# Sending k's column maxima through memory instead of through TensorE

## The chip, the cores and the metric

The kernel runs on one NeuronCore of a Trainium2 chip. The core has five engines with an instruction queue each: PE (TensorE; the profile shows its weight loads apart, as PEld), DVE (VectorE), ACT (ScalarE), POOL (GpSimd) and SP (SyncE, which here only starts transfers). Each engine works through its own queue in order and waits on semaphores for the others. The metric is device time in microseconds, from one launch to its end; lower is better.

## The reference

Linear attention over 8 batches x 8 heads, 576 positions and 64 columns per head, and behind it a mixer of two small networks. All of it is float32.

```python
q_s = q - np.max(q, axis=-1, keepdims=True)
q_s = np.exp(q_s)
q_s = q_s / (np.sum(q_s, axis=-1, keepdims=True) + 1e-09)
k_s = k - np.max(k, axis=2, keepdims=True)        # the maximum over the 576 positions
k_s = np.exp(k_s)
k_s = k_s / (np.sum(k_s, axis=2, keepdims=True) + 1e-09)
kv = np.einsum('bhsd,bhse->bhde', k_s, v)
attn = np.einsum('bhsd,bhde->bhse', q_s, kv)
...
xt = x.transpose(0, 2, 1)                          # x: attn, its heads side by side
h = np.maximum(xt @ w_tok1, 0.0) @ w_tok2
u = x + h.transpose(0, 2, 1)
h2 = np.maximum(u @ w_ch1, 0.0) @ w_ch2
out = u + h2
```

The softmax of k runs along the positions, so its maximum is one number per column of k.

## The kernel before, in words

Two heads of one batch are a unit, so that 2 x 64 columns fill 128 partitions. There are 32 units. For each the kernel loads q and k with the positions on the partitions (five chunks of 128 rows), k also transposed (`kt`, columns on the partitions), and v. Units 0 to 7 are the early ones; units 8 to 13 come next; from unit 14 on (`PAIRED` = 14), units are treated in pairs: `stage_kv` of both units of a pair stands at the pair's first place.

The second network (the channel network, `ch1` and `ch2`) works on groups of 512 rows. A group needs 12 steps, one for each 128 of the 1536 hidden channels. In a step, `ch1` does 12 matmuls of 512 columns into one bank of `ps_h` (L430). ACT empties that bank into `h2h` (L433), DVE into `h2l` (L434), the rest that `h2h` lacks, so that two reduced-precision products stand for a float32 one. `ch2` of the step before then does 12 matmuls into the four banks of `ps_o` (L442). After a group's last step `out_end` empties those four banks on DVE (L473, L474), and ACT starts the stores. The units' own stages are put between the steps: the dictionary `todo`, filled by `put`, says at which step, or half a step later, a stage is traced.

k's softmax is `softmax_k`. From unit 8 on it does this: DVE reduces `kt` along the row to one maximum per column, `mc`, one per partition (L237). The product needs those 128 numbers along the free axis, in every partition alike. So ACT scales the identity by `mc` into `dg` (L251), PE multiplies a matrix of ones with `dg` (L253; a float32 product, two instructions in the trace), and ACT copies the result from its bank to `mb` (L254). POOL subtracts `mb` from k (L255), and ACT takes the exponential (L256). `stage_kv` (L295) uses the result. `dg` and `mb` are one buffer each, `mc` has two, and `kt` has one (L154).

q's softmax (`softmax_q`) begins with a reduction on DVE that waits for q's load (L263), and ends with the split into `qh` and `ql`, the latter on POOL (L118). Then DVE and ACT turn q block by block (L344).

The order on each engine is not the order of the text. A planner (`schedule_with_timeline_sim=True`) takes the traced instructions, with their place in the text as priority, and writes each engine's queue by its own estimate of when things are ready. `tc.issue_after(ins)` adds an edge for it without a semaphore: instructions traced inside the block that stand on the engine of `ins` come behind `ins` in that engine's queue. `behind(...)` (L417) does so for a list of instructions, and `drained` (L432) holds the two emptyings, on ACT and on DVE, of the last `ch1` traced.

Of the kernel before, what the change touches and what calls it, by code (L numbers as in the profile page):

```python
# [8 lines left out]
F32 = mybir.dt.float32  # L9
F32R = mybir.dt.float32r  # L10
U32 = mybir.dt.uint32
AF = mybir.ActivationFunctionType
# [3 lines left out]
P = 128  # L16
# [4 lines left out]
def attn_mixer_kernel(ctx: ExitStack, tc: tile.TileContext, q, k, kt, v, wt, out, dims):  # L21
# [3 lines left out]
    nc = tc.nc  # L25
# [12 lines left out]
    PAIRED = NE + NJ + 2  # L38
# [5 lines left out]
    sm = ctx.enter_context(tc.tile_pool(name="sm", bufs=2))  # L44
# [6 lines left out]
    ident = const.tile([P, P], F32R, name="ident")  # L51
# [13 lines left out]
    ones = const.tile([P, P], F32, name="ones")  # L65
# [26 lines left out]
    dg = lay.tile([P, P], F32, name="dg")  # L92
    for i in range(3):
        slots[i][1] = lay.tile([P, NJ, CW], F32R, name=f"ul{i}")
    mb = lay.tile([P, P], F32, name="mb")
# [14 lines left out]
    Q = 32  # L110

    def f32(ap):
        return ap.bitcast(F32)
# [8 lines left out]
    def ps_unit(dtype=F32):  # L122

        pools = unit_banks[0]
        pool, name = pools[turn[0] % len(pools)]
        turn[0] += 1
        return pool.tile([P, 512], dtype, name=name)
# [102 lines left out]


    turned_k = []

    def softmax_k(u):
        ktt = u["kt"]
        mc = sm.tile([P, 1], F32, name="mc")
        nc.vector.tensor_reduce(mc, ktt, axis=AX.X, op=ALU.max)  # L237
        kx = u["k"]
        if u["early"]:
            nc.vector.tensor_scalar(mc, mc, -1.0, None, op0=ALU.mult)  # L240
            nc.scalar.activation(ktt, ktt, AF.Exp, bias=mc)
            t = ps_unit()
            for c in range(C):
                nc.tensor.transpose(t[:, c * P : (c + 1) * P], ktt[:, c * P : (c + 1) * P], f32(ident))
            nc.scalar.copy(kx[:, 0:C, :], t.rearrange("p (c d) -> p c d", c=C))
            t = ps_unit()
            turned_k.append(nc.tensor.transpose(t[:, 0:P], ktt[:, S0 : S0 + P], f32(ident)).ins)
            nc.scalar.copy(kx[:, C, :], t[:, 0:P])
            return

        nc.scalar.activation(dg, f32(ident), AF.Copy, scale=mc)  # L251
        t = ps_unit()
        nc.tensor.matmul(t[:, 0:P], ones, dg, start=True, stop=True)  # L253
        nc.scalar.copy(mb, t[:, 0:P])  # L254
        nc.gpsimd.tensor_tensor(kx, kx, mb.unsqueeze(1).broadcast_to([P, C1, P]), op=ALU.subtract)  # L255
        nc.scalar.activation(kx, kx, AF.Exp)  # L256

# [30 lines left out]
    def stage_kv(u):  # L288
        kx, vt = u["k"], v_of[u["n"]]
        kv = ps_unit()  # L290

        for c in range(C1):
            for h in range(2):
                hs = slice(h * D, (h + 1) * D)
                nc.tensor.matmul(kv[hs, 0 : D + 1], kx[:, c, hs], vt[:, c, h, :], start=(c == 0), stop=(c == C))  # L295

        if u["n"] != NE - 1 and u["n"] < PAIRED:
            load_v(u["n"] + 2 if u["n"] < NE else u["n"] + 1)
        rs = sm.tile([P, 1], F32, name="rs")
        nc.vector.tensor_scalar(rs, kv[:, D : D + 1], 1e-9, None, op0=ALU.add)  # L300
        nc.vector.reciprocal(rs, rs)
        kvf = kv_ring[u["n"] % len(kv_ring)]
        for h in range(2):
            hs = slice(h * D, (h + 1) * D)
            nc.scalar.activation(kvf[hs, hs], kv[hs, 0:D], AF.Copy, scale=rs[hs])
        u["kvf"] = kvf
        if not u["early"] and u["n"] < PAIRED:
            split_kv(u)

    def split_kv(u):  # L310
        kvf = u["kvf"]
        kvh = wk.tile([P, P], F32R, name="kvh")
        kvl = wk.tile([P, P], F32R, name="kvl")
        split(kvh, kvl, kvf, nc.vector)
        u["kvh"], u["kvl"] = kvh, kvl
# [67 lines left out]
    def stage_u(u, half):  # L383
        b, j = u["b"], u["j"]
        edge = (b + 1) * CW - b * S
        cut = min(max(edge, S - 320), 320)
        n0, n1 = ((0, cut), (cut, S))[half]
        N = n1 - n0
        ns = slice(n0, n1)
        t = ps_unit()  # L390
        if u["early"]:
            mm = [(u["kvf"], u["qt"][:, ns])]
        else:
            mm = [(u["kvh"], u["qth"][:, ns]), (u["kvh"], u["qtl"][:, ns]), (u["kvl"], u["qth"][:, ns])]
        for n in range(NT):
            mm += [
                (u["hh"][:, n, :], w2h[:, n, ns]),
                (u["hh"][:, n, :], w2l[:, n, ns]),
                (u["hl"][:, n, :], w2h[:, n, ns]),
            ]  # L400
        for i, (a, w) in enumerate(mm):
            nc.tensor.matmul(t[:, 0:N], a, w, start=(i == 0), stop=(i == len(mm) - 1))  # L402
        for g, a0, a1 in ((b, n0, min(n1, edge)), (b + 1, max(n0, edge), n1)):
            if a0 < a1:
                at = b * S + a0 - g * CW
                uh, ul = (x[:, j, at : at + a1 - a0] for x in uT[g])
                src = t[:, a0 - n0 : a1 - n0]
                emptied[:] = [
                    nc.scalar.copy(uh, src).ins,  # L409
                    nc.vector.tensor_tensor(ul, src, f32(uh), op=ALU.subtract).ins,  # L410
                ]


    drained = []

    @contextmanager
    def behind(instructions):  # L417
        with ExitStack() as stack:
            for ins in instructions:
                stack.enter_context(tc.issue_after(ins))  # L420
            yield
# [56 lines left out]
    units = {}  # L478

    def begin(n):  # L480
        if n < NU and n not in units:
            units[n] = load_unit(n // NJ, n % NJ)

    def soft(n):
        if n < NU:
            softmax_k(units[n])
            softmax_q(units[n])

    def pe_stages(n):
        def s1():  # L490
            stage_qT(units[n])
            stage_kv(units[n])

        def s2():
            stage_y(units[n])

        def s3():
            stage_h1(units[n])
            stage_u(units[n], 0)

        def s4():
            stage_u(units[n], 1)

        return s1, s2, s3, s4
# [66 lines left out]

    todo = {}


    def second_places():
        t = part.rearrange("p n c -> p (n c)")
        n = C1 * 2 * (D + 1)
        v_ring.append(v_places(t[:, 0:n].rearrange("p (c h e) -> p c h e", c=C1, h=2)))
        nc.gpsimd.memset(t[:, n : n + P], 0.0)
        kv_ring.append(t[:, n : n + P])  # L580
        load_v(PAIRED + 1)
# [6 lines left out]
    def put(at, fn):  # L588
        todo.setdefault(int(2 * at) / 2, []).append(fn)
# [4 lines left out]
    for n in range(NE, NU):  # L594
        b, j = divmod(n, NJ)
        s1, s2, s3, s4 = pe_stages(n)
        if b == 2:
            at = (n0 - 10, n0 - 9, n0 - 9, n0 - 7.5) if j == 0 else [n0 - 9.5 + 2 * j + x for x in (0, 0.5, 1, 1.5)]
            put(at[0], s1)
            put(at[0], lambda n=n: soft(n + 1))  # L600
            put(at[0] + 0.5, lambda n=n: begin(n + 2))
            for x, fn in zip(at[1:], (s2, s3, s4)):
                put(x, fn)
            continue
        at = n0 + (b - 3) * NF + 3 * j - 1
        if prev is not None:
            put(at, lambda n=prev: (stage_u(units[n], 0), stage_u(units[n], 1)))
        if n < PAIRED:
            put(at, lambda n=n: (stage_kv(units[n]), stage_y(units[n]), stage_qT(units[n])))
        elif n % 2 == 0:  # L610
            put(at, lambda n=n: (stage_kv(units[n]), stage_kv(units[n + 1]), load_v(n + 2), load_v(n + 3)))
            put(at, lambda n=n: (split_kv(units[n]), stage_y(units[n]), stage_qT(units[n])))
        else:
            put(at, lambda n=n: (split_kv(units[n]), stage_y(units[n]), stage_qT(units[n])))
        if n + 1 < PAIRED:
            put(at, lambda n=n: soft(n + 1))
        elif n + 1 < NU:
            put(at, lambda n=n: softmax_q(units[n + 1]))
        put(at + 0.5, lambda n=n: begin(n + 2))

        for m, x, y in ((n + 2, 0.5, 1.5),) if n < PAIRED else ((n + 2, 0.5, 1.5), (n + 3, 2, 3)) if n % 2 == 0 else ():
            if m < NU:
                put(at + x, lambda m=m: (begin(m), load_kt(units[m])))
                put(at + y, lambda m=m: softmax_k(units[m]))
        if n + 2 >= PAIRED and n + 2 < NU:
            put(at + 0.5, lambda n=n: load_q(units[n + 2]))
        if n + 1 == PAIRED:
            put(at - 1, second_places)
        put(at + 1.5, lambda n=n: stage_h1(units[n]))
        prev = n  # L630
# [88 lines left out]
```

## Time and profile before

| | us |
|---|---|
| median of three runs | 816.17 (814.79 to 816.81) |
| profiled execution | 816.05 |
| its span, first to last instruction | 814.2 |
| mean granted TensorE clock | 0.992 |

| engine | busy us | instructions |
|---|---|---|
| PE | 797.4 | 4512 |
| PEld | 678.8 | 4512 |
| DVE | 495.4 | 1104 |
| ACT | 338.2 | 898 |
| POOL | 84.2 | 72 |

A row of groups reads: line, engine, operation, tiles written and read, shape, count, then busy time, the mean of one in ns, and the idle time of the engine just before, with what ended it. A row of waits reads: who waited for whom, the sum in us, how often, the longest. A row of the timeline gives start and length in us, and in brackets the idle time before. Matmuls are pipelined, so a matmul's length in the profile is more than what it adds to the time; the difference of two starts shows that.

The 24 products of L253 start between 145.4 and 606.1 us; six belong to units 8 to 13, and the eighteen from 245.8 us on to units 14 to 31.

### The profile page before, as it was taken

How to read it: one execution, taken by the hardware profiler on the slowest of the kernel's cores; microseconds unless marked ns; L12 is line 12 of the kernel's file. 1: busy time of each engine (PE TensorE's matmuls, PEld its weight loads, DVE VectorE, ACT ScalarE, POOL GpSimd, SP SyncE). 2: the span in 40 equal slices, each digit the busy share in tenths (PEclk: the TensorE clock that was granted, in tenths of full speed). 3: DMA queues.
4: the chain of work that ended last, by engine and by line, in shares of the span. 5: the costliest groups of instructions: out<-in, count | busy, mean ns of one | idle time of the engine just before them, and what ended most of it. 6: DMA issues, size and time to landing. Idle time of an engine off the chain costs nothing.

```text
span 814.2 us, 12016 instructions
## 1 busy us (share of the span) xinstructions
PE 797.4 (98%) x4512; PEld 678.8 (83%) x4512; DVE 495.4 (61%) x1104; ACT 338.2 (42%) x898; POOL 84.2 (10%) x72
## 2 busy tenths in 40 slices
PE   7899999989999999999999999999999999999997
PEld 6688888878888888888888888888888888888886
DVE  6999998887786565855568464847475214113112
ACT  7976564448554343434444443434343311101110
POOL 1000000102121110201111020202020000000100
PEclk9999999999999999999999999999999999999999
DMA  9753433414324130413132212320120001001001
GB/s 298 246 161 94 149 111 107 147 59 124 93 64 130 39 103 9 139 33 95 32 91 88 79 49 79 101 69 26 27 103 17 1 1 53 0 1 52 0 1 52
DMA packets 60633, 63.55 MB, mean 78 GB/s; under 512 B 40864, under 2 KB 40992, under 8 KB 60576
## 3 DMA queue, kind: packets, MB, share of 16 engines
q1 hardware_dynamic: 55392, 53.36, 22.0%
q10 hardware_dynamic: 5184, 9.44, 3.1%
q8 instruction: 35, 0.57, 0.3%
q14 instruction: 22, 0.18, 0.1%
HBM read 53.35 MB, written 9.44 MB: 77 GB/s over the span
## 4 chain that ended last, share of the span: by engine, by line
PE 87%; DVE 6%; DMA 3%; ACT 2%; issue 1%; SPq 0%; DVEq 0%; ACTq 0%
PE ps_o L442 34%; PE ps_h L430 34%; PE ps_h L402 8%; PE ps_h L358 5%; PE ps_h L295 2%; DMA stg<-in_w 2%; PE ps_h L366 1%; PE ps_o L402 1%; DVE q_t L344 1%; ACT q_t L269 1%; DMA kt_t<-in_kt 1%; PE ps_o L358 1%; DVE cv_s L194 1%; DVE mc L237 1%; PE ps_h L253 1%
## 5 line engine op out<-in xcount | busy, mean ns | idle before, releaser
L430 PE MATMUL ps_h<-uh,cw 128*128 128x512 f32 x864 | 270.0, 392 | 0.4 <-DVE cw L118 0.4
L442 PE MATMUL ps_o<-h2h,cw 128*128 128x512 f32 x864 | 263.6, 394 | 2.3 <-DVE cw L118 2.2
L442 PEld LDWEIGHTS ps_o<-h2h,cw 128*128 128x128 f32 x864 | 161.1, 189 | 35.4 <-ACT h2h L433 2.5
L430 PEld LDWEIGHTS ps_h<-uh,cw 128*128 128x128 f32 x864 | 160.3, 188 | 33.1 <-DVE cw L118 0.8
L434 DVE SCALAR_TENSOR_TENSOR h2l<-ps_h,h2h 128x512 fp32r<-128x512 f32 x108 | 73.7, 682 | 175.9 <-ACT h2h L433 175.8
L433 ACT ACTIVATE h2h<-ps_h 128x512 fp32r<-128x512 f32 x108 | 64.4, 597 | 268.2 <-PE ps_h L430 251.6
L430 PE MATMUL ps_h<-ul,cw 128*128 128x512 f32 x432 | 168.4, 390 | 0.0
L442 PE MATMUL ps_o<-h2l,cw 128*128 128x512 f32 x432 | 160.9, 390 | 0.0
L430 PEld LDWEIGHTS ps_h<-ul,cw 128*128 128x128 f32 x432 | 81.1, 188 | 17.0
L442 PEld LDWEIGHTS ps_o<-h2l,cw 128*128 128x128 f32 x432 | 80.9, 188 | 16.4
L344 DVE COPY q_t<-cv_s 32x160 f32<-32x160 f32 (+1 forms) x264 | 66.0, 250 | 22.2 <-POOL ql L118 18.9
L118 POOL TENSOR_TENSOR ql<-q_t,qh 128x640 fp32r<-128x640 f32 x24 | 38.4, 1600 | 366.4 <-ACT qh L117 244.3
L255 POOL TENSOR_TENSOR k_t<-k_t,mb 128x640 f32<-128x640 f32 x24 | 38.3, 1594 | 187.1 <-ACT mb L254 187.1
L263 DVE TENSOR_REDUCE st<-q_t 128x10 f32<-128x640 f32 x32 | 26.1, 816 | 48.1 <-DMA q_t<-in_q 48.0
L344 ACT COPY q_t<-cv_s 32x128 f32<-32x128 f32 (+1 forms) x120 | 36.8, 307 | 2.1 <-DVE cv_s L336 0.7
L274 ACT ACTIVATE q_t<-q_t 128x640 f32<-128x640 f32 x24 | 17.7, 739 | 38.7 <-DVE q_t L273 37.7
L402 PE MATMUL ps_h<-w2h,hh 128*128 128x320 f32 (+1 forms) x112 | 33.4, 299 | 0.0
L402 PE MATMUL ps_h<-w2h,hl 128*128 128x320 f32 (+1 forms) x112 | 32.9, 299 | 0.3 <-DVE hl L374 0.2
L402 PE MATMUL ps_h<-w2l,hh 128*128 128x320 f32 (+1 forms) x112 | 33.0, 296 | 0.0
L409 ACT CAST uh<-ps_h 128x320 fp32r<-128x320 f32 (+4 forms) x76 | 25.0, 334 | 14.3 <-PE ps_h L402 9.8
L410 DVE TENSOR_TENSOR ul<-ps_h,uh 128x320 fp32r<-128x320 f32 (+4 forms) x76 | 27.5, 371 | 4.6 <-ACT uh L409 3.7
L278 DVE TENSOR_TENSOR q_t<-q_t,st 128x640 f32<-128x640 f32 x32 | 28.6, 895 | 0.8
(154 smaller groups left out, 1072.3 us busy)
## 6 DMA issues: line engine op xcount, KB each, us to landing
stg<-in_w SPq DMA_DIRECT2D x28, 512.0 KB, 3.9
kt_t<-in_kt SPq DMA_DIRECT2D x32, 320.0 KB, 3.0
q_t<-in_q SPq DMA_DIRECT2D x32, 320.0 KB, 3.4
out<-stg ACTq DMA_DIRECT2D x32, 256.0 KB, 2.2
k_t<-in_k SPq DMA_DIRECT2D x24, 320.0 KB, 3.6
v_t<-in_v SPq DMA_DIRECT2D x46, 128.0 KB, 2.9
part<-in_v SPq DMA_DIRECT2D x18, 128.0 KB, 2.6
out<-part ACTq DMA_DIRECT2D x4, 256.0 KB, 2.7
```

The source lines that it names most:

```text
L118: lo_eng.tensor_tensor(lo, src, f32(hi), op=ALU.subtract)
L255: nc.gpsimd.tensor_tensor(kx, kx, mb.unsqueeze(1).broadcast_to([P, C1, P]), op=ALU.subtract)
L263: nc.vector.tensor_reduce(st[:, 0, :], qt, axis=AX.X, op=ALU.max)
L278: nc.vector.tensor_tensor(qt, qt, st[:, 2, :].unsqueeze(2).broadcast_to([P, G, D]), op=ALU.mult)
L344: eng(qx[ys, 0:n, xs], turned[xs, 0:n, ys])
L358: nc.tensor.matmul(y[:, 0:TOK], a, w, start=(i == 0), stop=(i == len(mm) - 1))
L402: nc.tensor.matmul(t[:, 0:N], a, w, start=(i == 0), stop=(i == len(mm) - 1))
L410: nc.vector.tensor_tensor(ul, src, f32(uh), op=ALU.subtract).ins,
L430: nc.tensor.matmul(t, cw[f][x][:, n, :], w, start=(i == 0), stop=(i == 3 * NJ - 1))
L433: nc.scalar.activation(hh, t, AF.Relu).ins,
L434: nc.vector.scalar_tensor_tensor(hl, t, 0.0, f32(hh), op0=ALU.max, op1=ALU.subtract).ins,
L442: nc.tensor.matmul(o, cw[f][x][:, n, :], w, start=(first and i == 0), stop=(last and i == 2))
```

## The change

For units 14 to 31 the maxima take another way. The reduction writes its column into `dg[:, 0:1]` itself. One DVE instruction transposes the first 32 columns of `dg` in blocks of 32x32, so that the 128 maxima lie along four rows, 32 in each, in partitions 0, 32, 64 and 96. SP sends these four rows to a small tile in device memory (`row`, two buffers), and then reads that tile back into `mb` with the same 128 numbers to every partition. POOL's subtraction and ACT's exponential are as before. The scaling on ACT, the product on PE and the copy on ACT fall away for these units.

Besides, `softmax_k` of these units is traced inside `behind(drained)`: its instructions on DVE (reduction and transpose) come behind the step's `h2l`, and its instruction on ACT (the exponential) behind the step's `h2h`. SP's and POOL's instructions get no edge, since `drained` holds none of theirs.

```diff
+    dram = ctx.enter_context(tc.tile_pool(name="dram", bufs=2, space=bass.MemoryType.DRAM))
 
     def softmax_k(u):
         ktt = u["kt"]
-        mc = sm.tile([P, 1], F32, name="mc")
+        through = u["n"] >= PAIRED
+        mc = dg[:, 0:1] if through else sm.tile([P, 1], F32, name="mc")
         nc.vector.tensor_reduce(mc, ktt, axis=AX.X, op=ALU.max)
...
-        nc.scalar.activation(dg, f32(ident), AF.Copy, scale=mc)
-        t = ps_unit()
-        nc.tensor.matmul(t[:, 0:P], ones, dg, start=True, stop=True)
-        nc.scalar.copy(mb, t[:, 0:P])
+        if through:
+
+            nc.vector.transpose(dg[:, Q : 2 * Q], dg[:, 0:Q])
+            row = dram.tile([P // Q, Q], F32, name="row")
+            nc.sync.dma_start(row, dg[0:P:Q, Q : 2 * Q])
+            nc.sync.dma_start(mb, row.rearrange("(o x) q -> o (x q)", o=1).broadcast_to([P, P]))
+        else:
+            nc.scalar.activation(dg, f32(ident), AF.Copy, scale=mc)
+            t = ps_unit()
+            nc.tensor.matmul(t[:, 0:P], ones, dg, start=True, stop=True)
+            nc.scalar.copy(mb, t[:, 0:P])
         nc.gpsimd.tensor_tensor(kx, kx, mb.unsqueeze(1).broadcast_to([P, C1, P]), op=ALU.subtract)
         nc.scalar.activation(kx, kx, AF.Exp)
...
+    def after_step(fn, *args):
+        with behind(drained):
+            fn(*args)
...
-                put(at + y, lambda m=m: softmax_k(units[m]))
+                put(at + y, lambda m=m: after_step(softmax_k, units[m]))
```

## The prediction

> **What bounds the kernel now.** I read the page first, then the busy time by stage, then who waited for whom in the stage that the change touches.
>
> ```profile
> PE 797.4 (98%) x4512; PEld 678.8 (83%) x4512; DVE 495.4 (61%) x1104; ACT 338.2 (42%) x898; POOL 84.2 (10%) x72
> PE 87%; DVE 6%; DMA 3%; ACT 2%; issue 1%; SPq 0%; DVEq 0%; ACTq 0%
> ```
>
> TensorE is busy for 98% of the span, and the chain of work that ended last runs through it for 87%. The eighteen units work between 240 and 640 us, so that stage is asked alone:
>
> ```profile
> 0.00:240.00 240.00, 228.45 (x1361) 193.74 (x1362) 208.52 (x467) 148.67 (x443) 18.33 (x27) 0.98 0.44 137
> 240.00:640.00 400.00, 399.83 (x2383) 344.14 (x2382) 249.59 (x575) 167.91 (x416) 60.89 (x41) 1.00 0.23 68
> ```
>
> The columns are the window's length, then PE, PEld, DVE, ACT and POOL busy with their counts, the granted clock, the DMA share and GB/s. In 240 to 640 PE is busy 399.83 of 400 us at a granted clock of 1.00, while DVE is busy 249.59, ACT 167.91 and POOL 60.89. The waits of the weight loads in the same window:
>
> ```profile
> PEld ps_h L295 <- issue: 1.3, 7, 0.2
> PEld ps_o L442 <- ACT k_t L256: 0.6, 1, 0.6
> PEld ps_o L442 <- DVE stg L473: 0.2, 1, 0.2
> ```
>
> Only 0.8 us of 400 go to a wait for another engine. So in this stage the time is the sum of TensorE's instructions. Work taken off PE shortens it; work moved among the others is free until it makes PE wait.
>
> The Trainium skill speaks against this reading: "Trainium Kernel Development and Optimization", section Performance Expectations, calls matmul busy time a bad metric and takes the busy share of LDWEIGHTS instead. By that rule PE has room here, for its loads fill 344.14 of 400 us, and removing products could give nothing. The start times below disagree with it. The rule's result is the first rival.
>
> **What the change removes.** Per unit, one product of `ones` with `dg` on PE (two instructions), and on ACT the scaling of the identity (L251) and the copy to `mb` (L254). What a product occupies is read from starts, since durations overlap:
>
> ```profile
> 509.16 0.38 PE L253 MATMUL ps_h<-dg,ones 128*128 128x128 f32 x2
> 509.38 0.61 PE L366 MATMUL ps_h<-kvf,ys 128*128 128x128 f32 x4
> ...
> 517.11 0.62 PE L442 MATMUL ps_o<-h2h,cw 128*128 128x512 f32 x2
> 517.57 0.39 PE L442 MATMUL ps_o<-h2l,cw 128*128 128x512 f32 x1
> 517.79 0.39 PE L430 MATMUL ps_h<-ul,cw 128*128 128x512 f32 x1
> 518.02 0.38 PE L253 MATMUL ps_h<-dg,ones 128*128 128x128 f32 x2
> 518.16 0.71 PE L442 MATMUL ps_o<-h2h,cw 128*128 128x512 f32 x2
> 518.71 0.28 PE L402 MATMUL ps_h<-qth,kvh 128*128 128x256 f32 x1
> ```
>
> From the product's start to the next instruction's are 0.22 us at 509. At 518 they are 0.14, but the two matmuls behind it then take 518.71-518.16 = 0.55 where such a pair took 517.57-517.11 = 0.46, so 0.23 in all. I take 0.22; the low end is 0.14. Eighteen units: 18 x 0.22 = 4.0 us (2.5 to 4.1). The 512-column matmuls around follow each other at 0.23 us (517.57, 517.79, 518.02), with no hole into which this time could vanish.
>
> ACT loses 408 and 258 ns per unit:
>
> ```profile
> L237 DVE TENSOR_REDUCE mc<-kt_t 128x1 f32<-128x640 f32 x32 | 25.8, 805 | 4.4 <-DMA kt_t<-in_kt 3.2 <-ACT dg L251 1.2
> L336 DVE STREAM_TRANSPOSE cv_s<-q_t 128x640 f32<-128x640 f32 x24 | 20.2, 842 | 0.7
> L251 ACT ACTIVATE dg<-ident,mc 128x128 f32<-128x128 f32 x24 | 9.8, 408 | 0.2
> L254 ACT COPY mb<-ps_h 128x128 f32<-128x128 f32 x24 | 6.2, 258 | 4.8 <-PE ps_h L253 4.8
> L300 DVE TENSOR_SCALAR rs<-ps_h 128x1 f32<-128x1 f32 x27 | 4.0, 149 | 0.3
> ```
>
> That is 12.0 us off an engine idle for 232 of the 400 us: nothing on the path. One PSUM bank in use per unit falls away too; PE shows no wait for a bank here, so nothing again.
>
> **What it adds.** One DVE transpose of 128x32. The trace has none; it lies between the smallest DVE row above, 0.15 us, and the 128x640 transpose, 0.84. It is far nearer to the first in size: I take 0.2, so 3.6 us in all (2.7 to 15). Other work hides it: PE, which needs DVE's results later. The cover is the margin between an emptying (`h2l`) and PE's load of it, which I read below. Without cover it would cost these 3.6 us.
>
> Two transfers on SP per unit, 0.5 KB to memory and 64 KB back, the second waiting for the first. Nearest rows:
>
> ```profile
> out<-stg ACTq DMA_DIRECT2D x32, 256.0 KB, 2.2
> part<-in_v SPq DMA_DIRECT2D x9, 32.0 KB, 2.8
> k_t<-in_k SPq DMA_DIRECT2D x24, 320.0 KB, 3.6
> ```
>
> So 2.2 to 3.6 us each; I take 2.8, the smallest load's, and 5.6 for both. The Trainium skill's page "DMA: Bandwidth & Descriptors", section Rules for kernel authors, speaks against such transfers: under 64 KB one pays mostly overhead. The rows agree that small is not fast (2.8 us for 32 KB, 3.6 for ten times that), but by the rule too this is latency, and it costs time only where it ends a wait.
>
> **What it moves.** Each reduction must now stand behind the emptying of its step on DVE, and the exponential behind its step's `h2h` on ACT. I follow the pair prepared from 421 us on and used at 454:
>
> ```profile
> 421.40 0.68 DVE L434 SCALAR_TENSOR_TENSOR h2l<-ps_h,h2h 128x512 fp32r<-128x512 f32 x1
> ...
> 431.70 0.65 DVE L434 SCALAR_TENSOR_TENSOR h2l<-ps_h,h2h 128x512 fp32r<-128x512 f32 x1
> 432.28 0.80 DVE L237 TENSOR_REDUCE mc<-kt_t 128x1 f32<-128x640 f32 x1
> ...
> 437.60 0.82 DVE L263 TENSOR_REDUCE st<-q_t 128x10 f32<-128x640 f32 x1 [2.79 <-DMA q_t<-in_q]
> ...
> 444.32 0.68 DVE L434 SCALAR_TENSOR_TENSOR h2l<-ps_h,h2h 128x512 fp32r<-128x512 f32 x1
> ```
> ```profile
> 431.52 1.57 POOL L255 TENSOR_TENSOR k_t<-k_t,mb 128x640 f32<-128x640 f32 x1 [7.62 <-ACT mb L254]
> 437.65 1.57 POOL L118 TENSOR_TENSOR ql<-q_t,qh 128x640 fp32r<-128x640 f32 x1 [4.55 <-DMA q_t<-in_q]
> ```
> ```profile
> 454.03 0.74 PE L295 MATMUL ps_h<-v_t,k_t 128*64 128x65 f32 x18
> ```
>
> A reduction already stands right behind an `h2l` (432.28); the new order puts another unit's there. DVE's load in the crowded part therefore grows by the 0.2 us alone.
>
> First unit: `h2l` ends 422.1; +0.8 reduction, +0.2 transpose = 423.1; +5.6 = 428.7; POOL's subtraction 1.57 to 430.3; exponential 0.7 to 431.0. Second unit: reduction ends 433.1, transpose 433.3, transfers 438.9. POOL would do `ql` first (437.65 to 439.2), then k to 440.8; exponential to 441.5. PE wants both at 454.0: 12.5 us to spare, so the chain off PE costs nothing. That the chain misses its use altogether would need 9 us per transfer, which no row supports.
>
> SP is strictly in order, and the new transfers are two more waits in it:
>
> ```profile
> 427.73 5.70 SPq L155 DMA_DIRECT2D kt_t<-in_kt  x2
> 434.27 0.33 SPq L163 DMA_DIRECT2D q_t<-in_q  x1
> ```
>
> Behind them stand the next transposed k (one buffer, free only after the reduction) and q. The former has ten microseconds between the two reductions for a load of 3.6 us. q's is the second rival.
>
> **Sum.** The profiled execution took 816.05 us, 1.85 of it outside the span of 814.2; it lies 0.12 under the median of the runs, so it stands for them. 816.05 - 4.0 = 812.1. With the bounds of the product, 812.0 to 813.6. Should the 0.8 us of waits go in the new order, 811.3.
>
> **The rivals.**
>
> *Nothing is gained*: the removed products lay in PE's holes. For it the loads' 86% in the stage; against it the unbroken 0.23 us rhythm. Time 816.
>
> *q waits behind the second transfer.* If SP holds `mb`'s read ahead of q's load, q starts when the row has landed, 433.3+2.8 = 436.1 instead of 434.27, 1.8 later. DVE waits for exactly that load at 437.60, and the emptying at 444.32 is behind it. It ends 445.0; PE loads it here:
>
> ```profile
> 446.36 0.19 PEld L442 LDWEIGHTS ps_o<-h2l,cw 128*128 128x128 f32 x1
> ```
>
> The margin is 1.36, so PE would stall 0.5 us in a pair. Nine pairs as tight as this: 4.2, time 816.3; half of them: 814.2. I put it at 815. Against it: q is ready to issue at 434.3, before the read can be.
>
> *Slower: the exponential stands ahead of the next step's emptying on ACT.* ACT is in order too, and the new edge binds the exponential only to its own step's `h2h`. The next one:
>
> ```profile
> 427.39 0.60 ACT L433 ACTIVATE h2h<-ps_h 128x512 fp32r<-128x512 f32 x1 [1.73 <-DVE stg L474]
> ...
> 433.27 0.19 PEld L442 LDWEIGHTS ps_o<-h2l,cw 128*128 128x128 f32 x1
> ```
> ```profile
> 600.85 0.68 DVE L434 SCALAR_TENSOR_TENSOR h2l<-ps_h,h2h 128x512 fp32r<-128x512 f32 x1
> ...
> 608.97 0.19 PEld L442 LDWEIGHTS ps_o<-h2l,cw 128*128 128x128 f32 x1
> ```
>
> From the end of one `h2l`, the chain to the exponential's end takes 0.8+0.2+5.6+1.6+0.7 = 8.9, and `h2h` and `h2l` behind it 1.3 more: 10.2. At 422.1 the next `h2l` is wanted at 433.27, 11.2 later: no stall. In the last pair it is wanted 608.97-601.5 = 7.5 later: a stall of 2.7. It decides once chain and margin cross. The mean of 0 and 2.7 over nine pairs is 12 us, time 824; with 2.2 us per transfer 1.5 at the end, mean 0.75, 6.8 us, time 819. I put it at 821. For it: ACT already stood waiting in order for DVE before that `h2h`. Against it: the subtraction ends at 430.3 at the earliest, 2.9 us after `h2h` could run, so only an order planned with transfers under 1.4 us would place it so.
>
> **How the numbers follow.** About 0.3% (2.4 us) is what a measurement of this kernel can tell from no change. Forecast, 812.1 with its own range of 811.0 to 813.7: 0.54. The same with the waits gone, 811.3: 0.06. Nothing gained: 0.08. q's wait: 0.14. The exponential ahead: 0.18. The first two are faster: 0.60; the next two lie within 0.3%: 0.22; the last is slower: 0.18. The range runs from 811.0 to 819.0, up to the low end of the slower rival; outside it lie most of that rival and a little below.
>
> **What would show it.** PE and PEld should count 4476 instead of 4512, ACT 862, DVE 1122; L253 should have 12 instructions. PE in the stage should stay without waits: a PE wait for `h2l` or `h2h` there would prove one of the last two rivals, with DVE's wait for q grown over 2.8 us at its place, or an `h2h` standing behind `k_t` on ACT. The two transfers' time to landing should be 2.2 to 3.6 us, and POOL's k subtraction should start about 6.5 us after its `h2l`. A transfer over 4 us, or PE waits of more than 1.6 us in all, would make the prediction wrong.

## The result and the profile after

The changed kernel takes 824.87 us (median of 6 runs, 820.75 to 830.41) where the kernel before took 815.36 on the same chips (6 runs): a ratio of 1.0118, 95% interval 1.0096 to 1.0139. It is slower by 1.2%; 812.1 had been forecast, and the time lies above the range. The profiled execution took 825.79 us, of which 824.0 are span. The diff moves line numbers: the reduction is now L239, the transpose L255, the two transfers L257 and L258, POOL's subtraction L264, the exponential L265, `ch1` L439, `h2h` L442, `h2l` L443, `ch2` L451.

The busy times and the chain of waits, from the page of the kernel after:

```profile
PE 797.0 (97%) x4476; PEld 675.6 (82%) x4476; DVE 494.9 (60%) x1122; ACT 326.3 (40%) x862; POOL 84.7 (10%) x72
PE 51%; DVE 10%; DMA 4%; issue 1%; ACT 1%; SPq 0%; POOL 0%; DVEq 0%
```

The counts are those predicted: 36 instructions fewer on PE and on ACT, 18 more on DVE. The chain that ended last runs through PE for 51% where it was 87%; its shares add up to 67%, so a third of the span is not followed, and it can't be read as finely as that of before. The stage again, as length, then PE, PEld, DVE, ACT, POOL busy, clock, DMA share, GB/s:

```profile
240.00:640.00 400.00, 391.02 (x2278) 333.46 (x2278) 248.51 (x580) 151.37 (x367) 59.25 (x40) 0.99 0.25 73
```

PE is idle for 9.0 us of 400 where it was idle for 0.2, and gets through 2278 instructions instead of 2383. DVE, ACT and POOL are busy less than before, in part because the same 400 us now hold less of the work. The waits of PE in the same stretch (sum in us, times, longest):

```profile
PE ps_o L451 <- DVE h2l L443: 3.9, 4, 1.3
PE ps_o L451 <- ACT h2h L442: 3.6, 3, 1.7
PE ps_h L367 <- DVE h2l L443: 1.5, 1, 1.5
```

These eight waits are the 9.0 us, and all of them are for the two emptyings.

To size the loss, a ruler is better than the span: single profiled executions start their first `ch2` step up to 2.3 us apart, long before anything differs. The 25th and the 79th step of `ch2` bracket nearly all of the changed units, and seventeen of the eighteen products. First the starts of both in the kernel before, then in the kernel after:

```profile
249.22 0.62 PE L442 MATMUL ps_o<-h2h,cw 128*128 128x512 f32 x2
...
644.25 0.62 PE L442 MATMUL ps_o<-h2h,cw 128*128 128x512 f32 x2
```
```profile
249.06 0.62 PE L451 MATMUL ps_o<-h2h,cw 128*128 128x512 f32 x2
...
653.99 0.62 PE L451 MATMUL ps_o<-h2h,cw 128*128 128x512 f32 x2
```

Before: 644.25 - 249.22 = 395.03 us. After: 404.93, so +9.90. Outside the bracket next to nothing is lost.

**Where it goes.** The pair that the prediction followed, now on ACT (start, length, idle time before and what ended it):

```profile
434.43 0.74 ACT L265 ACTIVATE k_t<-k_t 128x640 f32<-128x640 f32 x1 [7.81 <-POOL k_t L264]
435.07 0.58 ACT L442 ACTIVATE h2h<-ps_h 128x512 fp32r<-128x512 f32 x1
...
445.89 0.74 ACT L265 ACTIVATE k_t<-k_t 128x640 f32<-128x640 f32 x1 [3.76 <-POOL k_t L264]
447.06 0.74 ACT L283 ACTIVATE q_t<-q_t 128x640 f32<-128x640 f32 x1 [0.43 <-DVE q_t L282]
447.71 0.58 ACT L442 ACTIVATE h2h<-ps_h 128x512 fp32r<-128x512 f32 x1
```

An exponential stands ahead of an `h2h` twice in the pair, the first time directly. The first waits 7.81 us for POOL; the `h2h` behind it reads a bank that PE had filled at 429.88 and runs at 435.07, 5.2 us late. PE had that much to spare. The second exponential ends at 446.6, q's L283 follows, and the `h2h` at 447.71 reads a bank that was full at 440.75, 7.0 us late; for this one PE waits. In each of the other five pairs in which PE waits from 350 us on, the late `h2h` (3.7 to 6.3 us) stands behind an exponential too. At 495, 540 and 585 us PE waits for `h2l` alone, which DVE reaches 1.0 to 2.3 us after its `h2h`, behind the copies of q and a reduction. DVE shows how the lateness passed from the first to the second:

```profile
423.59 0.81 DVE L239 TENSOR_REDUCE dg<-kt_t 128x1 f32<-128x640 f32 x1
...
427.44 0.20 DVE L255 STREAM_TRANSPOSE dg<-dg 128x32 f32<-128x32 f32 x1
...
435.68 0.69 DVE L443 SCALAR_TENSOR_TENSOR h2l<-ps_h,h2h 128x512 fp32r<-128x512 f32 x1 [3.40 <-ACT h2h L442]
436.29 0.81 DVE L239 TENSOR_REDUCE dg<-kt_t 128x1 f32<-128x640 f32 x1
...
442.18 3.99 DVE L353 COPY q_t<-cv_s 32x160 f32<-32x160 f32 x11
```

The first reduction ends at 424.4, but its transpose runs only at 427.44, 3.0 us later: other work of DVE (`out_end`'s L482 and L483, a reduction of q) stands between them. And the second reduction is bound behind the `h2l` of the late `h2h`. It had stood at 432.28 and now stands at 436.29. So the second chain starts late because the first one was late on ACT. In the kernel before the chain had a lead: counted off in order, the maxima of the two products at 421.6 and 430.4 had been reduced at 345.0 and 381.7, a lead that the edges take away. On SP and on POOL:

```profile
427.66 0.55 SPq L257 DMA_DIRECT2D row<-dg  x1
429.30 0.32 SPq L258 DMA_DIRECT2D mb<-row  x1
...
438.30 0.33 SPq L163 DMA_DIRECT2D q_t<-in_q  x1
438.73 0.53 SPq L257 DMA_DIRECT2D row<-dg  x1
441.35 0.33 SPq L258 DMA_DIRECT2D mb<-row  x1
```
```profile
432.83 1.56 POOL L264 TENSOR_TENSOR k_t<-k_t,mb 128x640 f32<-128x640 f32 x1 [15.53 <-DMA mb<-row]
438.64 1.57 POOL L118 TENSOR_TENSOR ql<-q_t,qh 128x640 fp32r<-128x640 f32 x1 [4.25 <-ACT qh L117]
444.25 1.60 POOL L264 TENSOR_TENSOR k_t<-k_t,mb 128x640 f32<-128x640 f32 x1 [4.04 <-DMA mb<-row]
```

From the first transfer's issue to POOL's start are 432.83 - 427.66 = 5.2 us, and 5.5 the second time (4.6 to 6.0 over all eighteen). POOL's second subtraction now stands behind `ql`, where before both subtractions came first (422.34 and 431.52, then 437.65), and it meets DVE's copies of q: the eleven at 442.18 take 3.99 us. PE, last:

```profile
446.26 0.39 PE L439 MATMUL ps_h<-ul,cw 128*128 128x512 f32 x1
448.34 0.96 PE L451 MATMUL ps_o<-h2h,cw 128*128 128x512 f32 x3 [1.69 <-ACT h2h L442]
...
451.36 1.05 PE L451 MATMUL ps_o<-h2h,cw 128*128 128x512 f32 x2
452.21 0.63 PE L451 MATMUL ps_o<-h2l,cw 128*128 128x512 f32 x1
452.64 1.04 PE L439 MATMUL ps_h<-uh,cw 128*128 128x512 f32 x2
```

PE starts `ch2` 448.34 - 446.26 = 2.08 us after the last `ch1` matmul where 0.23 is usual. Soon behind the wait three matmuls take 452.64 - 451.36 = 1.28 us, 0.43 each, half the usual rate, and so it stays for some three microseconds. A matmul at half rate costs 0.2 us more. Over the bracket, waits measured from start to start come to 10.2 us, sixteen matmuls at half rate (nine after 449, seven after 630) to 16 x 0.2 = 3.2, and seventeen products fall away with 17 x 0.22 = 3.7: 10.2 + 3.2 - 3.7 = 9.7 of the 9.90.

### The profile page after: what moved, and what is told of

Same layout as the page of the kernel before. It is cut to its first block, busy times and chain, and to the rows that moved or that the text cites. A ratio compares the mean times of both kernels' runs of the same rounds, so it can differ in the third digit from the quotient of the medians.

```text
span 824.0 us, 11983 instructions
## 1 busy us (share of the span) xinstructions
PE 797.0 (97%) x4476; PEld 675.6 (82%) x4476; DVE 494.9 (60%) x1122; ACT 326.3 (40%) x862; POOL 84.7 (10%) x72
## 4 chain that ended last, share of the span: by engine, by line
PE 51%; DVE 10%; DMA 4%; issue 1%; ACT 1%; SPq 0%; POOL 0%; DVEq 0%
PE ps_o L451 21%; PE ps_h L439 20%; PE ps_h L411 5%; DMA q_t<-in_q 4%; DVE q_t L353 3%; PE ps_h L367 3%; PE ps_h L304 1%; DVE st L272 1%; DVE stg L482 1%; DVE q_t L282 1%; DVE h2l L443 1%; DVE dg L239 1%; DVE st L284 1%; DVE qtl L118 1%; DVE stg L483 1%
## 5 line engine op out<-in xcount | busy, mean ns | idle before, releaser
L451 PE MATMUL ps_o<-h2h,cw 128*128 128x512 f32 x864 | 265.0, 397 | 6.0 <-ACT h2h L442 3.9
L439 PE MATMUL ps_h<-uh,cw 128*128 128x512 f32 x864 | 270.3, 393 | 0.0
L451 PEld LDWEIGHTS ps_o<-h2h,cw 128*128 128x128 f32 x864 | 161.5, 190 | 40.3 <-ACT h2h L442 8.0
L439 PEld LDWEIGHTS ps_h<-uh,cw 128*128 128x128 f32 x864 | 161.1, 189 | 32.4
L443 DVE SCALAR_TENSOR_TENSOR h2l<-ps_h,h2h 128x512 fp32r<-128x512 f32 x108 | 73.8, 683 | 184.9 <-ACT h2h L442 184.8
L439 PE MATMUL ps_h<-ul,cw 128*128 128x512 f32 x432 | 168.5, 390 | 0.0
L451 PE MATMUL ps_o<-h2l,cw 128*128 128x512 f32 x432 | 162.9, 396 | 4.1 <-DVE h2l L443 4.1
L442 ACT ACTIVATE h2h<-ps_h 128x512 fp32r<-128x512 f32 x108 | 64.2, 594 | 250.0 <-PE ps_h L439 233.6
L451 PEld LDWEIGHTS ps_o<-h2l,cw 128*128 128x128 f32 x432 | 81.6, 190 | 23.5 <-DVE h2l L443 6.8
L439 PEld LDWEIGHTS ps_h<-ul,cw 128*128 128x128 f32 x432 | 81.3, 188 | 17.0
L353 DVE COPY q_t<-cv_s 32x160 f32<-32x160 f32 (+1 forms) x264 | 74.2, 281 | 23.1 <-POOL ql L118 19.7
L264 POOL TENSOR_TENSOR k_t<-k_t,mb 128x640 f32<-128x640 f32 x24 | 38.7, 1611 | 226.0 <-DMA mb<-row 134.2
L265 ACT ACTIVATE k_t<-k_t 128x640 f32<-128x640 f32 x24 | 17.8, 740 | 74.7 <-POOL k_t L264 74.5
L283 ACT ACTIVATE q_t<-q_t 128x640 f32<-128x640 f32 x24 | 17.8, 741 | 30.9 <-DVE q_t L282 30.8
L418 ACT CAST uh<-ps_h 128x64 fp32r<-128x64 f32 (+4 forms) x76 | 25.1, 335 | 11.2 <-PE ps_h L411 6.6
L367 PE MATMUL ps_h<-w1h,qh 128*128 128x256 f32 x96 | 27.6, 287 | 1.5 <-DVE h2l L443 1.5
```

What stands on the lines that cost most here:

```text
L353: eng(qx[ys, 0:n, xs], turned[xs, 0:n, ys])
L367: nc.tensor.matmul(y[:, 0:TOK], a, w, start=(i == 0), stop=(i == len(mm) - 1))
L439: nc.tensor.matmul(t, cw[f][x][:, n, :], w, start=(i == 0), stop=(i == 3 * NJ - 1))
L442: nc.scalar.activation(hh, t, AF.Relu).ins,
L443: nc.vector.scalar_tensor_tensor(hl, t, 0.0, f32(hh), op0=ALU.max, op1=ALU.subtract).ins,
L451: nc.tensor.matmul(o, cw[f][x][:, n, :], w, start=(first and i == 0), stop=(last and i == 2))
```

## The experiments

What the trace after shows is one order of events; what causes the loss has several candidates: the way through memory itself, the edges, the place of the exponential in ACT's queue, the lateness of the chain, POOL's meeting with the copies. The runs take them one by one. Each edit is against the changed kernel unless it says otherwise; "bracket" is the time between the 25th and the 79th step of `ch2`, 395.03 us before and 404.93 after. The kernel before took 815.06 to 815.73 beside each group of runs, so medians of different groups may be subtracted.

### The rows without the edges

```diff
-                put(at + y, lambda m=m: after_step(softmax_k, units[m]))
+                put(at + y, lambda m=m: softmax_k(units[m]))
```

> The maxima go through memory as in the changed kernel, but without the edges that hold each unit's reduction behind its step's h2l and its exponential behind h2h. Theory 'in-order queue' (the exponential stands in ACT's queue ahead of an h2h and waits there for the transfers, which in turn hold h2l and PE): the reduction may now run as early as the buffers allow, so where the planner uses that, the chain is early and the time is near 812; where the second transfer still ends behind the place the planner gave the exponential, PE waits remain. Theory 'edge' (the edges themselves cost the time by holding the reduction): 812, and no PE wait for h2h. Theory 'transfers' (two transfers per unit disturb the other loads whatever their place): 820 or more, as with the edges.

Measured: 824.78 us (4 runs), ratio to before 1.0097 (1.0059 to 1.0135). No faster than with the edges, but the loss lies elsewhere. The bracket takes 402.20 us, and 8.8 are lost on the kernel before between its 25th and its 31st step alone. DVE and PE there:

```profile
285.13 0.82 DVE L239 TENSOR_REDUCE dg<-kt_t 128x1 f32<-128x640 f32 x1 [2.22 <-DMA kt_t<-in_kt]
...
286.12 0.65 DVE L443 SCALAR_TENSOR_TENSOR h2l<-ps_h,h2h 128x512 fp32r<-128x512 f32 x1
...
288.92 0.82 DVE L239 TENSOR_REDUCE dg<-kt_t 128x1 f32<-128x640 f32 x1 [2.15 <-DMA kt_t<-in_kt]
```
```profile
286.82 1.35 PE L304 MATMUL ps_h<-part,k_t 128*64 128x65 f32 x20 [2.58 <-DVE h2l L443]
...
290.19 0.58 PE L367 MATMUL ps_h<-w1h,qh 128*128 128x256 f32 x1 [2.02 <-DVE ul L419]
```

Without edges DVE's queue holds the reductions of several units one after another; the last of the eighteen starts at 321.0 us, in the kernel after at 616.7. The two shown wait over 2 us each for a load into the one `kt` buffer, with an emptying behind the first. That is the same fault, an instruction that waits for a transfer ahead of an emptying, on another engine. From the 31st to the 79th step, with the last reduction at 321, this kernel takes 348.8 us, where the kernel after takes 359.3 and the kernel before 350.4. So there the edges do cost the time, by making the chain late; without them the reductions crowd the start and cost as much in another place. One caution: the writes of `row` run many units ahead of its reads, though it has two buffers, so what a unit subtracts may be another unit's maxima. A softmax does not depend on the number subtracted, and only the times of this run are used. The 820 or more of theory 'transfers' fits the number here; the last two runs below keep all the transfers and are fast, so it falls.

### The edge on the kernel before

```diff
-                put(at + y, lambda m=m: softmax_k(units[m]))
+                put(at + y, lambda m=m: after_step(softmax_k, units[m]))
```

The edit is against the kernel before.

> The product on PE stays, only the edges are added for units 14 to 31. Theory 'edge': about as slow as the changed kernel, plus the 4.0 us that the products cost, so 825 or more. Theory 'in-order queue': the chain behind the reduction is here dg 0.4, product 0.2, mb 0.3, subtraction 1.6 us instead of two transfers, so the exponential is ready before the next h2h: 815 to 818, with PE waits below 2 us in all.

Measured: 830.75 us (4 runs), ratio 1.0179 (1.0145 to 1.0214). DVE and PE around 515:

```profile
511.40 0.82 DVE L263 TENSOR_REDUCE st<-q_t 128x10 f32<-128x640 f32 x1 [4.94 <-DMA q_t<-in_q]
...
515.63 0.68 DVE L473 TENSOR_TENSOR stg<-ps_o,uh 128x512 f32<-128x512 f32 x1
```
```profile
516.46 0.70 PE L442 MATMUL ps_o<-h2h,cw 128*128 128x512 f32 x2 [2.08 <-DVE stg L473]
...
518.13 0.49 PE L253 MATMUL ps_h<-dg,ones 128*128 128x128 f32 x2 [0.67 <-ACT dg L251]
```

Theory 'in-order queue' had 815 to 818 here and missed; the 825 or more of theory 'edge' came true. DVE's queue now holds q's reduction, waiting 4.94 us for its load, ahead of `out_end`, whose L473 PE then waits for. And the reduction of k behind the emptying comes so late that PE, which has the product in its own queue, waits for `dg` (0.67 us here). Beside the same edges the way through memory is worth 830.75 - 824.87 = 5.9 us. Neither half of the change alone is a gain.

### No transfers: POOL subtracts what stands in `dg`

```diff
-            row = dram.tile([P // Q, Q], F32, name="row")
-            nc.sync.dma_start(row, dg[0:P:Q, Q : 2 * Q])
-            nc.sync.dma_start(mb, row.rearrange("(o x) q -> o (x q)", o=1).broadcast_to([P, P]))
...
-        nc.gpsimd.tensor_tensor(kx, kx, mb.unsqueeze(1).broadcast_to([P, C1, P]), op=ALU.subtract)
+        top = dg if through else mb
+        nc.gpsimd.tensor_tensor(kx, kx, top.unsqueeze(1).broadcast_to([P, C1, P]), op=ALU.subtract)
```

The spreading of the maxima is left out here: each partition subtracts its own row of `dg`. All else is kept, the edges and the order of tracing with it.

> The changed kernel without its two transfers: POOL subtracts what lies in dg instead of mb, so that the subtraction still waits for the reduction and the transpose, but the maxima are not spread (this part of the computation is left out). Theories 'in-order queue' and 'shared port': without the 5 us of latency the subtraction ends before the next h2h and before the copies: 811 to 813, the 4.0 us of the products. Theory 'edge': still 818 or more, for the reduction is held as before.

Measured: 812.4 us (10 runs), ratio 0.9962 (0.9945 to 0.9979); bracket 391.86, -3.17. ACT in the same pair:

```profile
429.48 0.74 ACT L263 ACTIVATE k_t<-k_t 128x640 f32<-128x640 f32 x1 [3.06 <-DVE st L283]
431.15 0.60 ACT L440 ACTIVATE h2h<-ps_h 128x512 fp32r<-128x512 f32 x1 [0.93 <-PE ps_o L449]
```

The exponential is still ahead of the `h2h`, but its data come early enough: this `h2h` is 1.7 us late instead of 5.2, and that behind the start of two stores. Elsewhere in the stage an `h2h` still comes up to 4.6 us late behind an exponential, but PE waits only 0.9 us in all. This is the forecast's time. The edges are kept here, so the late chain alone costs next to nothing; it takes the transfers' latency of 5 us on top of it, paid in ACT's queue or behind it.

### The exponential traced later

```diff
-        nc.scalar.activation(kx, kx, AF.Exp)
+        if not through:
+            nc.scalar.activation(kx, kx, AF.Exp)
+
+    def exp_k(u):
+        nc.scalar.activation(u["k"], u["k"], AF.Exp)
...
+                put(at + y + 2, lambda m=m: after_step(exp_k, units[m]))
```

> The changed kernel with the exponential alone put two steps later, behind that later step's h2h. Theory 'in-order queue': ACT's waits for POOL's k subtraction (74.5 us in the changed kernel) fall under 5 us, h2h follows its ch1 again, and the time comes down to 812 to 815. Theory 'shared port' (POOL's later subtraction falls on DVE's copies of q, and the h2l behind them is late): the copies beside the subtraction still take 1.6 us instead of 0.25, PE still waits for h2l once in a pair, and 817 to 821 remain.

Measured: 815.78 us (10 runs), ratio 1.0003 (0.9988 to 1.0018). Two steps are too late for unit 15: its exponential came behind the use of its k, so that this unit was computed from the differences. The next run mends that with one step for the first pair:

```diff
-                put(at + y + 2, lambda m=m: after_step(exp_k, units[m]))
+                put(at + y + (2 if n >= PAIRED else 1), lambda m=m: after_step(exp_k, units[m]))
```

> As e3, with unit 15's exponential ahead of its use (in e3 it stood behind it). Theory 'in-order queue' and the clock aside, the time should be that of e3, 815 to 816, with PE's remaining waits (3 to 4 in all) for h2l alone and none for h2h.

Measured: 816.54 us (10 runs), ratio 1.0019 (1.0004 to 1.0035); bracket 395.96. PE's waits in 240 to 640:

```profile
PE ps_o L455 <- DVE h2l L447: 3.0, 4, 1.5
PE ps_h L371 <- DVE h2l L447: 1.6, 1, 1.6
```

The waits for `h2h` are gone, and 824.87 - 816.54 = 8.3 us with them, by moving one instruction a unit in ACT's queue (the bracket of this run also has none of the 3.2 us of half rate). But 4.6 us of waits for `h2l` remain, more than the products gave, and the exponentials still wait 24.8 us for POOL, not the under 5 expected, though for the most part with no `h2h` right behind. The times of both runs, 815.78 and 816.54, lie between the ranges of the two theories. At 446, where PE waits 0.5 us, what DVE does late ahead of `h2l` is not a copy but the subtraction of q, which met POOL's subtraction of k and took 2.23 us instead of 0.82:

```profile
439.72 2.23 DVE L286 TENSOR_TENSOR q_t<-q_t,st 128x640 f32<-128x640 f32 x1
```

### Another POOL instruction on the copies, in the kernel before

```diff
+        if u["n"] >= PAIRED:
+            hi = qh[:, 0:C, :]
+            nc.gpsimd.tensor_tensor(hi, f32(hi), zero.unsqueeze(2).broadcast_to([P, C, P]), op=ALU.add)
```

The edit is against the kernel before. The added instruction, behind each `ql`, adds zero to `qh`. It is there to make POOL busy while DVE copies q.

> The kernel before with one POOL instruction more per unit from 14 on, put right behind ql: it adds zero to the first four chunks of qh, and nothing waits for it but the next y. It starts when DVE's copies of q start. Theory 'shared port': the copy that meets it takes 1.2 us or more instead of 0.25, the emptying behind the copies is some 1.1 us later, and where its margin is 0.7 to 1.6 us PE waits: 815.5 to 820. If the port is free the copies stay at 0.25 us and the time at 815.7.

Measured: 816.28 us (10 runs), ratio 1.0011 (1.0000 to 1.0022). The copies of this kernel among the groups (mean of one in ns behind the busy time):

```profile
L349 DVE COPY q_t<-cv_s 32x160 f32<-32x160 f32 (+1 forms) x264 | 72.9, 276 | 23.1 <-POOL ql L120 19.9
```

They take 72.9 us, about what they take in the kernel after (74.2; before 66.0), and PE shows no wait for it. The test is milder than the sum looks: nine of its twelve long copies took 0.97 to 1.09 us and not the 1.6 of the kernel after. Longer copies of this size are absorbed by the margins.

The traces settle the rest of this rival. From 240 to 640 us, the time by which DVE's instructions beside POOL's exceed their group's median (by 0.25 us or more) adds up to 13.4 us in the kernel before and 14.3 in the kernel after; in the kernel before it falls on other instructions. It is 4.1 us in the next run (817.73) and 11.6 in the last (810.57). So the meetings with POOL do not set the time by their sum. They can add to a wait where an emptying is late already.

### The chain traced earlier, the exponential left ahead

```diff
-        for m, x, y in ((n + 2, 0.5, 1.5),) if n < PAIRED else ((n + 2, 0.5, 1.5), (n + 3, 2, 3)) if n % 2 == 0 else ():
+        for m, x, y in ((n + 2, 0.5, 1.5),) if n < PAIRED else ((n + 2, -0.5, 0.5), (n + 3, 1, 1.5)) if n % 2 == 0 else ():
```

> The changed kernel with its chains traced earlier (first unit one step, second 1.5 steps) and the exponential left in softmax_k, so that it still stands in ACT's queue ahead of an h2h. Theory (the loss is the time by which the subtraction is late when ACT comes to the exponential): with the chain earlier both subtractions come ahead of both ql again, fewer copies meet POOL, but ACT still stops at each exponential for the transfers, since the edge moves with the chain: the exponential of the earlier step now stands ahead of that step's next h2h. 816 to 822, PE waits for h2h and h2l of 3 to 8 us, ACT's wait for k_t over 40 us. Rival (how early the chain starts is what counts, the exponential's place in the queue does not): under 814.5 as in the run with both, PE waits under 2 us. Second rival (only the place counts): 824 to 826.

Measured: 817.73 us (10 runs), ratio 1.0029 (1.0013 to 1.0044); bracket 395.21. ACT's largest wait, then POOL and DVE in the pair:

```profile
ACT k_t L265 <- POOL k_t L264: 73.2, 15, 9.4
```
```profile
423.46 1.71 POOL L264 TENSOR_TENSOR k_t<-k_t,mb 128x640 f32<-128x640 f32 x1 [4.64 <-DMA mb<-row]
434.31 1.58 POOL L264 TENSOR_TENSOR k_t<-k_t,mb 128x640 f32<-128x640 f32 x1 [9.13 <-PE ps_h L411]
439.74 1.57 POOL L118 TENSOR_TENSOR ql<-q_t,qh 128x640 fp32r<-128x640 f32 x1 [3.85 <-ACT qh L117]
```
```profile
443.54 2.72 DVE L353 COPY q_t<-cv_s 32x160 f32<-32x160 f32 x11
```

ACT stands as long behind POOL's subtraction as in the changed kernel (73.2 us; there 72.0 in the same view), and yet 7.1 us come back. Both subtractions precede `ql` again and eleven copies take 2.72 instead of 3.99, and an exponential holds up only one `h2h` of this pair. What counts is whether the wait outlasts the margin of the `h2h` behind it, not its length on ACT.

### Both: earlier chain, later exponential

The two edits above together, the exponential 2.5 steps behind its reduction (one step in the first pair).

> The changed kernel with the exponential later, and besides load, reduction and transfers of each pair put one step (first unit) and one and a half (second unit) earlier, so that POOL does both k subtractions ahead of both ql, as in the kernel before. Theory 'in-order queue' plus 'shared port': no copy of q beside a k subtraction in most pairs, DVE's copies back under 0.28 us on average, PE waits under 1.5 us in all, 811 to 813, faster than the kernel before by 0.4%. If the port does not matter: no better than e3, 815 to 816.

Measured: 813.6 us (12 runs), ratio 0.9971 (0.9957 to 0.9985); bracket 391.50, -3.53. That is 0.6 above the range expected, and 0.3% under the kernel before. With this the four corners are there: 824.87 with neither edit, 816.54 with the later exponential (two steps there, not 2.5), 817.73 with the earlier chain, 813.6 with both. One PE wait is left, 1.4 us in the first pair. ACT there:

```profile
258.97 0.74 ACT L269 ACTIVATE k_t<-k_t 128x640 f32<-128x640 f32 x1 [7.05 <-POOL k_t L264]
259.62 0.58 ACT L446 ACTIVATE h2h<-ps_h 128x512 fp32r<-128x512 f32 x1
```

Again an exponential that waits, ahead of an `h2h`.

### The first pair too

```diff
-        for m, x, y in ((n + 2, 0.5, 1.5),) if n < PAIRED else ((n + 2, -0.5, 0.5), (n + 3, 1, 1.5)) if n % 2 == 0 else ():
+        for m, x, y in ((n + 2, 0.5, 1),) if n == PAIRED - 2 else ((n + 2, -0.5, 0.5),) if n < PAIRED else ((n + 2, -0.5, 0.5), (n + 3, 1, 1.5)) if n % 2 == 0 else ():
...
-                put(at + y + (2.5 if n >= PAIRED else 1), lambda m=m: after_step(exp_k, units[m]))
+                put(at + y + (2.5 if n >= PAIRED else 2), lambda m=m: after_step(exp_k, units[m]))
```

The edit is against the kernel with both. Unit 14's reduction is traced half a step earlier and its exponential half a step later, which binds it to the next step's `h2h`; unit 15's reduction comes a step earlier.

> As the run that put the chain a step earlier and the exponential later (813.6), and the same now for the first pair, units 14 and 15, whose places lie behind ordinary units: unit 14's exponential one step later, unit 15's chain one step earlier. Theory (what is left of the loss sits where a pair's second exponential stands ahead of an h2h): the PE wait of 1.4 us at 259 goes, nothing else changes, 812.2, between 811.5 and 813.2, and 0.4% under the kernel before. Rival (the wait at 259 comes from the crowd of DVE there, ordinary unit and pair together, whatever the exponential's place): 813.6 again, the wait moved by a step.

Measured: 810.57 us (5 runs, 809.61 to 811.96), where the kernel before took 815.06 beside it: ratio 0.9938 (0.9924 to 0.9953). It beats both kernels. Its bracket, the exponentials among the groups, and the read of the row among the transfers (last number: us to landing):

```profile
249.75 0.61 PE L455 MATMUL ps_o<-h2h,cw 128*128 128x512 f32 x2
...
640.09 0.62 PE L455 MATMUL ps_o<-h2h,cw 128*128 128x512 f32 x2
```
```profile
L269 ACT ACTIVATE k_t<-k_t 128x640 f32<-128x640 f32 x18 | 13.2, 733 | 1.9 <-POOL k_t L264 1.8
```
```profile
mb<-row SPq DMA_DIRECT2D x18, 64.0 KB, 3.3
```

640.09 - 249.75 = 390.34, that is -4.69: 3.7 for the bracket's seventeen products, 0.3 for the kernel before's late start of `ch2` at 600 us, and 0.7 spread over many starts that no single cause explains. The eighteen exponentials wait 1.8 us for POOL in all. The way through memory is no faster here (4.5 to 10.1 us from the first issue to POOL's start); PE waits for nothing behind it. The median lies 0.9 us below the range expected of it; in the bracket the step from the run before is -1.16, as expected of a wait of 1.4. Of the other 1.9 us between the two medians, 0.55 lies between the kernel before's own medians (815.61 and 815.06), and the mean granted clock of the runs was higher here, 0.9952 against 0.9935; what more there is, is not settled.

## Why the prediction was wrong, point by point

**What bounds the kernel: right.** The bracket without waits is shorter by what PE was spared and 1.0 us more.

**The removed product, 4.0 us: right.** The bracket, with seventeen products worth 3.7, gains 3.2 us without the transfers (812.4 for the 812.1 forecast, with 0.9 us of waits in it) and 4.7 where every wait is gone, and there the weight loads fill 344.15 of the 400 us, as before: the rival by which nothing would be gained falls. No run takes ACT's 12.0 us off alone; this sum leaves at most 1.0 us for them.

**The transpose, 0.2 us: right**, 0.20 measured. **The transfers, 5.6 for both: right**, 5.2 and 5.5 from issue to POOL in this pair.

**The step that failed is "PE wants both at 454.0: 12.5 us to spare, so the chain off PE costs nothing".** It measured the chain against the last user of its result and not against what stands behind each of its instructions in a queue. The first exponential ended at 435.2 and the second at 446.6, both well ahead of the use; neither product of k ever waited. The `h2h` behind them had only the margin of its own `ch2`: 5.2 us late was still in time, 7.0 was not. Over the bracket such lateness cost 10.2 us of waits on PE and 3.2 us of half rate, where the forecast had nothing.

**The chain's times were too early, too.** The forecast had the first subtraction end at 430.3; it ended at 434.4: the reduction started 1.5 us later than put, 3.0 us of DVE's other work stands between reduction and transpose, which I had put back to back, and the transfers gave 0.4 back. POOL's subtraction was to start about 6.5 us after its `h2l`; it started 9.2 and 7.9 after. The second reduction was to end at 433.1; it ended at 437.1, since the `h2l` it is bound to was itself held up through the first exponential. The edge fed the first unit's lateness into the second, a loop that the forecast, pair member by pair member, did not have.

**The slower rival is what happened**, with an exponential ahead of an `h2h` on ACT. Its price of 819 to 824 was close to 824.87, in good part by luck. It took one round at a time and gave the pair at 421 us no stall; there PE loses 1.85 us. It had neither the loop nor the half rate, and its stalls came to 6.8 to 12 us where 10.2 of waits and 3.2 of half rate were measured. The argument by which I gave it 0.18, that "only an order planned with transfers under 1.4 us would place it so", fell: in the second unit the exponential stands ahead of the next `h2h`. In the first it lets the next one (426.01) pass and stands ahead of the one after. What the planner assumed of the transfers no trace shows, so why it chose this order stays open; that the order on the chip cannot be inferred from real latencies is plain. That place and lateness both matter is shown by the corners (place alone changed: 816.54; lateness alone: 817.73) and by the run without transfers, where the exponential still precedes an `h2h`, most of the lateness is gone, and the time is 812.4. These edits are not perfectly single: the planner writes all queues anew for each, which is why I read the order in each trace.

**q's wait behind the second transfer did not come.** In the pair followed, q's load (438.30) is issued just ahead of the second pair of transfers (438.73), and DVE waits 2.59 us for it where it waited 2.79.

**The test named in the prediction** told right: an `h2h` behind `k_t` on ACT, PE waits of more than 1.6 us.

## What to carry to other kernels

Before an instruction gets a longer wait, look at what stands behind it in its engine's queue and take that instruction's margin, not that of the result's user. A latency moved off the bottleneck engine is free only if the in-order engines reach its consumer after it has arrived: issue the chain earlier and the consumer later, as two edits, and look at the order in the trace, not in the text. With an edge that ties one chain's start to another's end, lateness travels; follow two rounds, not one, and count the lead that the old order gave.

## What the runs showed of the hardware

**A copy on DVE that starts while POOL subtracts waits it out.** A copy takes about 0.25 us; those that began under a POOL subtraction took 1.59 on average in the kernel after (nine of the 264; three before), about POOL's own 1.56 to 1.60, and beside the POOL instruction that adds zero, mostly of about 1.05 us, they took 0.97 to 1.09. A subtraction on DVE grew too (2.23 us for 0.82, above). The reductions did not: 21 of them met a POOL instruction in the kernel before and took 0.81 us like the others. The Trainium skill, "SBUF — State Buffer", section Who interferes with whom, says that DVE and GpSimd share a port pair which one instruction holds alone, and that copies can need it while reductions on this chip never do; the trace agrees.

**After a gap of some two microseconds PE can run at half its rate.** In the kernel after, the 512-column matmuls follow each other at 0.43 us instead of 0.23 for some 3 us (shown at 451.36), soon after a gap of 2.08 us between two starts, and again after two gaps of 1.32 and 1.07 us close together at 628. The granted clock, third from the end of this row, halves with it:

```profile
450.00:453.50 3.50, 3.50 (x11) 2.69 (x10) 2.10 (x4) 0.00 (x0) 0.00 (x0) 0.52 0.00 0
```

Nine such matmuls cost 1.8 us, which doubles the price of the first of these gaps. It does not always happen: in the two later-exponential runs gaps of 2.25 and 1.90 us left no such matmul. A cleaner sample lies ahead of the changed stage: each of the eleven profiled executions has one gap of 2.1 to 2.5 us near 169 us. Half rate follows in seven of them, the kernel before among them, and not in the other four. The Trainium skill, "TensorE: Matmul & The Clock Gate", Part 1 (The HAM clock gate), puts the drop behind an idle window of about 3.4 us that runs free of the kernel; here gaps of 2.1 to 2.5 us were at times enough. That the drop depends on where the window falls would fit these counts, but no run tests it.

The spread of the changed kernel's runs goes with the clock: from 820.75 us at a mean granted clock of 0.997 to 830.41 at 0.988. Its fastest execution is the best look at the loss without half rate: the kernel before took 813.85 to 814.60 in its executions at 0.997, so 6 to 7 us remain, as 9.90 - 3.2 = 6.7 has it.
